# A linear-attention block and a gated MLP on one Trainium2 core: the second half of one weight matrix is loaded on another engine's DMA queue

## The chip, the cores and the metric

The kernel runs on one core of a Trainium2 chip. The metric is the device time of one execution in microseconds (us). Before the change it is 220.55 us, the median of three runs (220.51 to 220.61). A profile of a further execution shows where the time goes.

## What is computed

One layer: a layer norm, then two branches on the same normalised tokens, and a sum with the input. Branch A is linear attention with learned softmax features (32 heads of 16), branch B a gated MLP without an activation function. There are 2048 tokens of width 512, and the MLP is 1792 wide. All tensors are bf16.

```python
x = A_x                                   # [1, 2048, 512]
xn = layernorm(x)                         # mean and variance over the 512
q, k, v = split(xn @ wqkv)                # 32 heads of 16
phi = lambda t: concat(softmax(t @ w_phi), softmax(-(t @ w_phi)))
kv = phi(k).T @ v;  z = phi(k).sum(tokens)
attn = (phi(q) @ kv) / (phi(q) @ z + 1e-6)
mlp = ((xn @ w_gate) * (xn @ w_up)) @ w_down
out = x + attn @ wo + mlp
```

## The kernel before

The tokens are cut into 16 tiles of 128 (`n`), and four tiles make a group (`T`). TensorE (PE) does all projections with 128x512 matmuls; ScalarE (ACT) does the exponentials and many copies out of PSUM; VectorE (DVE) does sums, reciprocals and the products of gate and up; GpSimd (POOL) does the softmax scaling and small scalars; SyncE (SP) only issues DMAs. The order on every engine is written out by hand (`manual_schedule`, L100): each engine executes its instructions in the order of the program text.

All weights are loaded once, at the start, and stay in SBUF. Two engines issue the loads, each on a hardware queue of its own. In the profile q1 is SP's queue and q10 is ACT's.

- On SP (L95 to L97, then L106 to L115): token tile 0 (`dma_x(0, 1)`, "x0" below, 128 KB), token tiles 2 and 3 together (`dma_pair(2)`, "the pair", 256 KB), the second half of the value weights `wv` (contraction chunks 2 and 3, L97, 256 KB), then the first 256 columns of the gate weights `wg` and of the up weights `wu` (256 KB each), `wphi`, the next 384 columns of `wg` and `wu`, a transposing load `wT2` of the key weights (L109), token tiles 4 to 7, the rest of `wg` and `wu`, tiles 8 to 15, `wd` and `wo`.
- On ACT (L103 to L105): after an activation that loads the table, token tile 1 ("x1", 128 KB) and the first half of `wv` (chunks 0 and 1, 256 KB).

The DMAs share eight semaphores in rotation. A DMA whose semaphore is taken by an earlier one waits on the issuing engine until that one has landed. In the program before, `wT2` (L109) waits in this way for the second half of `wv`.

The first four token tiles are treated apart. They are centred by DVE (`sub_sum`), transposed on PE (`lt`), and the value projection of tiles 0, 1 and 2 is cut into two halves (`first_v`, L366 to L369): first the contraction chunks 0 and 1, which need only the first half of `wv`, and later chunks 2 and 3. The text from L399 to L413 sets PE's order: `first_v(0, (0, 1))`, the transposes of tile 2, `first_v(1, (0, 1))`, `first_v(2, (0, 1))`, then `first_v(0, (2, 3))`, which is the first matmul that reads the second half of `wv`, then the transposes of tile 3, the second halves of tiles 1 and 2, and tile 3. The accumulators of tiles 0 and 1 appear as `kv` in the profile (they borrow those two banks), the others as `pv`.

After that PE runs the first MLP units (`ffn`, L278: 4 gate and 4 up matmuls each), the fold of `wphi` into the key weights (`fold`, L230), the key projections, and from tile 4 on the main loop (L447). Tiles 4 to 15 get their normalised transpose `xnT` from ACT and a transposing DMA on SP's queue (`apply` in `ln_block`, L203 to L207), which stands on that queue behind all the weight loads. The first reader of `xnT` for tile 4 is `vproj(4)` (L450).

Of the kernel before, what the change touches and what calls it, by code (L numbers as in the profile page):

```python
# [21 lines left out]
def kernel(  # L22
# [12 lines left out]
    nc = tc.nc  # L35
# [6 lines left out]
    DC = D // P  # L42
# [35 lines left out]
    def dma_x(lo, hi, eng=nc.sync):  # L78
        eng.dma_start(out=xall[:, lo:hi, :], in_=x_view[:, lo:hi, :])  # L79

    def dma_pair(n, eng=nc.sync):
        eng.dma_start(out=xall[:, n:n + 2, :], in_=pair(x_rows, n))  # L82

    def dma_cols(eng, w, src, lo, hi, at=0):
        eng.dma_start(out=w[:, :, lo - at:hi - at], in_=src[:, lo:hi].rearrange("(c p) f -> p c f", p=P))

    def dma_wv(lo, hi, eng):
        eng.dma_start(out=wv[:, lo:hi, :],
                      in_=A_wqkv[lo * P:hi * P, 2 * D:3 * D].rearrange("(c p) f -> p c f", p=P))

    def dma_gu(lo, hi):
        dma_cols(nc.sync, wg, B_w_gate, lo, hi)
        dma_cols(nc.sync, wu, B_w_up, lo, hi)

    dma_x(0, 1)  # L95
    dma_pair(2)
    dma_wv(2, DC, nc.sync)  # L97

    ET = mybir.EngineType
    ctx.enter_context(tc.manual_schedule(engines={ET.PE, ET.DVE, ET.Activation, ET.Pool, ET.SP}))  # L100
# [2 lines left out]
    nc.scalar.activation(out=first[:], in_=ones[:, 0:1], func=AF.Exp, scale=1.0)  # L103
    dma_x(1, 2, nc.scalar)
    dma_wv(0, 2, nc.scalar)  # L105
    dma_gu(0, 2 * P)  # L106
    nc.sync.dma_start(out=wphi[:], in_=A_w_phi.rearrange("(c h) d f -> (h d) c f", c=DC))
    dma_gu(2 * P, 5 * P)
# [429 lines left out]
```

## Time and profile before

| What | Value |
|---|---|
| median of three runs | 220.55 us |
| the profiled execution | 221.2 us |
| its span, from the first to the last instruction | 219.5 us |
| PE busy | 215.7 us, 98% of the span |
| DVE, ACT, POOL busy | 64%, 41%, 34% |
| HBM read / written | 8.67 MB / 2.10 MB |
| packets on SP's queue q1 / ACT's queue q10 | 47952 / 416 |
| granted TensorE clock | 1.0 throughout |

The span is 1.7 us shorter than the time of that execution; the rest lies outside the first and last instruction. PE is busy nearly all the time by this count, but a matmul's recorded end is modelled, so short stalls between matmuls hide in it. They are read from the distance between the starts of matmuls: a 128x512 matmul follows the one before it after 0.216 us when nothing holds it. DMA packets are counted on all 16 DMA engines together; a DMA has landed when each of them has added its one to the DMA's semaphore.

### The profile page before, as it was taken

The numbers are of one execution on the slowest core, as the hardware profiler recorded it, in microseconds if no ns is written. First come the engines' busy times: TensorE is split into PE (matmuls) and PEld (weight loads), VectorE is DVE, ScalarE is ACT, GpSimd is POOL, SyncE is SP. The second block draws the span as 40 slices with busy tenths as digits, with TensorE's granted clock in tenths as the row PEclk, the third lists the DMA queues.
The fourth block names the chain that finished last, engine by engine and source line by source line (L and its number), as shares of the span: only waits on it lengthen the run. The fifth ranks groups of instructions, "written<-read, shape, count | busy, mean of one in ns | idle before, by whom it ended". The sixth has DMA issues, their size and how long they took to land.

```text
span 219.5 us, 3491 instructions
## 1 busy us (share of the span) xinstructions
PE 215.7 (98%) x1291; PEld 103.4 (47%) x1291; DVE 141.1 (64%) x242; ACT 89.2 (41%) x159; POOL 74.1 (34%) x71
## 2 busy tenths in 40 slices
PE   8999999999999999999999999999999999999995
PEld 3444445454444444444554444444444444454443
DVE  4868866786598757667499773197655745454321
ACT  5445586459665875465444222231232322100000
POOL 2450853363348463736135433033023033000000
PEclk9999999999999999999999999999999999999999
DMA  5999997103202231202018445214451431412201
GB/s 189 267 268 365 378 237 147 25 0 51 48 0 49 51 72 23 48 3 48 1 26 97 97 101 115 51 24 96 96 73 26 96 72 28 94 50 72 70 28 48
DMA packets 48385, 19.91 MB, mean 91 GB/s; under 512 B 37488, under 2 KB 48240, under 8 KB 48368
## 3 DMA queue, kind: packets, MB, share of 16 engines
q1 hardware_dynamic: 47952, 19.29, 38.8%
q10 hardware_dynamic: 416, 0.39, 0.5%
q8 instruction: 10, 0.16, 0.3%
q14 instruction: 7, 0.06, 0.1%
HBM read 8.67 MB, written 2.10 MB: 49 GB/s over the span
## 4 chain that ended last, share of the span: by engine, by line
PE 95%; DMA 3%; SPq 0%; DVE 0%; issue 0%
PE g L287 22%; PE fin L303 22%; PE u L291 22%; PE fin L306 6%; PE k L249 6%; PE q L249 6%; PE pv L249 5%; DMA wv<-in_A_wqkv_dram 3%; PE kv L343 2%; PE ab L477 2%; PE pq L238 1%; PE kv L249 0%; SPq L82 0%; SPq L79 0%; DVE o_sb L313 0%
## 5 line engine op out<-in xcount | busy, mean ns | idle before, releaser
L291 PE MATMUL u<-xnT,wu 128*128 128x512 bf16 x224 | 57.5, 379 | 0.0
L287 PE MATMUL g<-xnT,wg 128*128 128x512 bf16 x224 | 57.5, 379 | 0.0
L295 DVE TENSOR_TENSOR hT<-u,g_sb 128x512 bf16<-128x512 f32 x56 | 37.0, 666 | 24.2 <-PE u L291 16.0
L266 POOL TENSOR_TENSOR phiq<-e,rsum 128x1024 bf16<-128x1024 f32 x16 | 30.9, 1933 | 63.5 <-DVE rsum L264 56.0
L262 DVE TENSOR_REDUCE sums<-e 128x64 f32<-128x1024 f32 x32 | 38.9, 1216 | 20.3 <-ACT e L259 20.3
L294 ACT CAST g_sb<-g 128x512 bf16<-128x512 f32 x56 | 32.9, 587 | 46.8 <-PE g L287 46.6
L303 PE MATMUL fin<-wd,hT 128*128 128x512 bf16 (+2 forms) x238 | 51.1, 366 | 0.0
L266 POOL TENSOR_TENSOR phik<-e,rsum 128x1024 bf16<-128x1024 f32 x16 | 30.9, 1932 | 40.0 <-DVE rsum L264 34.0
L291 PEld LDWEIGHTS <-wu 128*128 128x128 bf16 x224 | 21.9, 98 | 26.4
L303 PEld LDWEIGHTS <-hT 128*128 128x128 bf16 x238 | 22.4, 98 | 24.7
L287 PEld LDWEIGHTS <-wg 128*128 128x128 bf16 x224 | 21.1, 98 | 23.9
L249 PEld LDWEIGHTS <-xnT 128*128 128x128 bf16 x192 | 17.4, 98 | 18.5 <-ACT xnT L219 0.7
L313 DVE TENSOR_TENSOR o_sb<-fin,xall 128x512 bf16<-128x512 f32 (+2 forms) x13 | 8.5, 651 | 20.5 <-PE fin L306 20.5
L264 DVE RECIPROCAL rsum<-sums 128x64 f32<-128x64 f32 x32 | 17.7, 553 | 3.1
L306 PE MATMUL fin<-wo,oT 128*128 128x512 bf16 (+2 forms) x68 | 16.6, 366 | 0.0
L249 PE MATMUL k<-W1k,xnT 128*128 128x512 bf16 x64 | 16.4, 379 | 0.0
L249 PE MATMUL q<-W1q,xnT 128*128 128x512 bf16 x64 | 16.4, 378 | 0.0
L258 ACT ACTIVATE e<-q 128x512 f32<-128x512 f32 x12 | 7.2, 597 | 22.2 <-PE q L249 22.2
L249 PE MATMUL pv<-wv,xnT 128*128 128x512 bf16 x56 | 14.4, 379 | 0.0
L490 DVE TENSOR_TENSOR otok<-ab,rden 128x512 bf16<-128x512 f32 x16 | 11.1, 692 | 0.6
L335 ACT CAST vt<-pv 128x512 bf16<-128x512 f32 x12 | 7.0, 587 | 10.2 <-PE pv L249 10.2
L166 DVE BATCH_NORM_STATS2 stats<-xall 128x6 f32<-128x512 bf16 x16 | 10.6, 664 | 0.0
(62 smaller groups left out, 131.8 us busy)
## 6 DMA issues: line engine op xcount, KB each, us to landing
out_dram<-o_sb SPq DMA_DIRECT2D x15, 128.0 KB, 2.0
wd<-in_B_w_down_dram SPq DMA_DIRECT2D x1, 1792.0 KB, 15.7
xall<-in_A_x_dram SPq DMA_DIRECT2D x1, 1024.0 KB, 11.8
wg<-in_B_w_gate_dram SPq DMA_DIRECT2D x1, 640.0 KB, 9.1
wu<-in_B_w_up_dram SPq DMA_DIRECT2D x1, 640.0 KB, 10.2
xall<-in_A_x_dram SPq DMA_DIRECT2D x1, 512.0 KB, 4.4
wg<-in_B_w_gate_dram SPq DMA_DIRECT2D x1, 512.0 KB, 5.2
wu<-in_B_w_up_dram SPq DMA_DIRECT2D x1, 512.0 KB, 6.2
```

The source lines that it names most:

```text
L166: nc.vector.bn_stats(out=stats[:], in_=xall[:, n, :])
L249: nc.tensor.matmul(ps, lhsT=xnT[:, j, n * P:(n + 1) * P], rhs=w[:, j, :], start=(j == 0), stop=(j == DC - 1))
L262: nc.vector.tensor_reduce(out=sums[:], in_=ev, axis=AX.X, op=ALU.add)
L264: nc.vector.reciprocal(out=rsum[:].rearrange("p a b -> p (a b)"), in_=sums[:])
L266: nc.gpsimd.tensor_tensor(out=phi[:].rearrange("p g (x f) -> p (g x) f", f=DH), in0=ev, in1=rsum[:].to_broadcast((P, 2 * H, DH)), op=ALU.mult)
L287: nc.tensor.matmul(gps, lhsT=wg[:, c, f * P:(f + 1) * P], rhs=xnT[:, c, T * TT:(T + 1) * TT], start=(c == 0), stop=(c == DC - 1))
L291: nc.tensor.matmul(ups, lhsT=wu[:, c, f * P:(f + 1) * P], rhs=xnT[:, c, T * TT:(T + 1) * TT], start=(c == 0), stop=(c == DC - 1))
L294: nc.scalar.copy(out=g_sb[:], in_=gps)
L295: nc.vector.tensor_tensor(out=hTs[T][:, f, :], in0=ups, in1=g_sb[:], op=ALU.mult)
L303: nc.tensor.matmul(ps, lhsT=hTs[T][:, f, t4 * P:(t4 + 1) * P], rhs=wd[:, f, lo:lo + w], start=(f == 0), stop=False)
L306: nc.tensor.matmul(ps, lhsT=oTs[n][:, c, :], rhs=wo[:, c, lo:lo + w], start=False, stop=(c == DC - 1))
L490: nc.vector.tensor_tensor(out=o_tok[:].rearrange("p (b h d) -> p b h d", b=2, d=DH), in0=abv[:, :, :, 0:DH], in1=rden[:].to_broadcast((P, ...
```

## The change

The load of the second half of `wv` is taken from SP's queue, where it stood third, and put on ACT's queue, behind the first half. Nothing else in the text changes. PE, DVE and POOL have the same instructions in the same order. ACT has one DMA more, SP one less. Because the eight semaphores are handed out in order, some of them change hands: `wT2` (L109 before) now waits for the first part of `wg` to land instead of the second half of `wv`.

```diff
     dma_x(0, 1)
     dma_pair(2)
-    dma_wv(2, DC, nc.sync)
...
     dma_x(1, 2, nc.scalar)
     dma_wv(0, 2, nc.scalar)
+    dma_wv(2, DC, nc.scalar)
     dma_gu(0, 2 * P)
```

## Prediction

> **What bounds the kernel now.** I read the chain of waits first, since PE's 98% hides short stalls.
>
> ```profile
> 7.58 0.04 issue
> 7.62 0.59 PE kv L249 x2
> ...
> 28.97 0.25 PE kv L343 x8
> ...
> 33.54 0.26 PE kv L343 x8
> 33.80 1.03 PE pv L249 x4
> 34.83 0.86 PE k L249 x4
> ```
>
> Columns: start, length, what. From 7.62 us to the end the chain is PE alone, and before that it is the landing of `wv`. Two places are not at full pace. At 7.62 PE starts `first_v(0, (2, 3))`, 0.04 us after the second half of `wv` has landed (7.58). The matmul before it started at 7.18, so without a wait the next would have started at 7.18 + 0.22 = 7.40: PE loses 0.22 us. At 33.80 four matmuls of `vproj(4)` take 1.03 us where four others take 0.86: 0.17 us lost. That matmul reads `xnT` of tile 4, whose transposing DMA was issued at 26.93 and landed 6.8 us later, at 33.73. Everywhere else in the chain the pieces have their nominal length, so the time after 33.8 us is fixed work. Hence the end is set by the later of two things: PE's own arrival at `vproj(4)` (33.63 now) and the landing of `xnT` 4 (PE goes on at 33.80).
>
> The second thing to read is the start of the two queues.
>
> ```profile
> 0.79 0.39 SPq L79 DMA_DIRECT2D xall<-in_A_x_dram  x1
> 0.84 0.39 ACTq L79 DMA_DIRECT2D xall<-in_A_x_dram  x1
> 1.24 0.41 SPq L82 DMA_DIRECT2D xall<-in_A_x_dram  x1
> 1.27 0.46 ACTq L88 DMA_DIRECT2D wv<-in_A_wqkv_dram  x1
> 1.70 0.43 SPq L88 DMA_DIRECT2D wv<-in_A_wqkv_dram  x1
> 2.18 0.47 SPq L85 DMA_DIRECT2D wg<-in_B_w_gate_dram  x1
> ```
>
> So the order of issue is x0, x1, the pair, `wv` first half, `wv` second half, `wg`. Now the packets per queue, in the stretches 3.25 to 3.5, 4.0 to 4.25 and 4.75 to 5.0 us (packets, MB, their time as a share of 16 engines), and all packets from 5.5 to 6.5 us:
>
> ```profile
> q1 hardware_dynamic: 48, 0.10, 100.8%
> q10 hardware_dynamic: 1, 0.00, 0.2%
> ```
> ```profile
> q10 hardware_dynamic: 95, 0.10, 108.3%
> ```
> ```profile
> q1 hardware_dynamic: 70, 0.07, 79.7%
> ```
> ```profile
> DMA packets 558, 0.29 MB, mean 292 GB/s; under 512 B 16, under 2 KB 558, under 8 KB 558
> ```
>
> At 3.25 SP's queue moves the pair and ACT's queue stands still, although the first half of `wv` had been issued by 1.73. At 4.0 only ACT's queue moves, although SP's third load had been issued by 2.13. From 4.75 only SP's moves. The two queues are not served side by side here: the DMAs are served one after another in the order in which they were issued, whichever queue they are on, even where the issues are 0.03 us apart (1.24 and 1.27).
>
> ```profile
> wv<-in_A_wqkv_dram SPq DMA_DIRECT2D x1, 256.0 KB, 5.9
> wg<-in_B_w_gate_dram SPq DMA_DIRECT2D x1, 256.0 KB, 6.3
> ```
>
> The last column is us from issue to landing: `wv` second half 1.70 + 5.9 = 7.6, `wg` first part 2.18 + 6.3 = 8.48.
>
> **The change, part by part.** *SP's third issue goes.* It took 0.43 us and a gap of 0.05, so every later issue on SP that is not held by a wait comes 0.48 us earlier: `wg` at 1.70 instead of 2.18, `wu` at 2.21, `wphi` at 2.76, and so on. No engine waits for these issues themselves.
>
> *ACT gets a third issue* at 1.27 + 0.46 + 0.04 = 1.77, for about 0.46 us (the row of the first half, same shape). The next thing in ACT's order is the first `junk` sum, which starts at 3.58 when x1 has landed. The issue ends at 2.23, so 1.35 us of waiting covers it; the one activation before it runs at 2.08 behind the table load. Cost nothing; without that cover it would be 0.46 us on the sum of tile 1.
>
> *The order of service changes.* This is the term that decides. `wg` is now issued at 1.70 and the second half of `wv` at 1.77. By the order seen above `wg` is served first and `wv` second. Both are 256 KB, so they swap places: `wv` lands where `wg` landed, at 8.48, and PE resumes 0.04 us later, at 8.52 instead of 7.62, **+0.90 us**. A second way gives the same: 256 KB (0.262 MB) of `wg` at the 292 GB/s of the stretch 5.5 to 6.5 take 0.90 us, and that is what is put ahead of `wv`. Queued behind the waiting matmul on PE are the transposes of tile 3, the rest of the value projections and all MLP units; ACT, DVE and POOL follow PE there (the copy of tile 3's transpose at 8.47, the value copies from 9.39), so the whole front moves by 0.90. `wg`, needed by PE at 9.78 (then 10.68), lands about 7.6. No loss there.
>
> *What takes some of it back.* At 33.63 + 0.90 = 34.53 PE comes to `vproj(4)`, whose `xnT` landed at 33.73. The 0.17 us that PE now waits there vanish. So the end moves by 0.90 - 0.17 = **+0.73 us**, if the landing of `xnT` 4 stays. It stands behind the same weight bytes on SP's queue. `wT2` waits for whichever of the two loads is served first: `wv` before (landed 7.58, `wT2` issued at 7.59), `wg` after (again about 7.6), so the rest of the stream starts as before. And it may come 0.8 us later without being felt.
>
> *Bounds.* The landing is the uncertain number, since it goes by the slowest of 16 DMA engines. The trace records each increment of a DMA's semaphore: for the second half of `wv` 15 of the 16 had come by 6.45 and the last at 7.58; for `wg` 7.64 and 8.48. If that one late engine were not late, `wv` in second place would land at 7.64, PE would resume at 7.68, and PE's 0.06 us would vanish in the wait at 33.6: no change. If it lost another 0.4 us (a single 1 KB packet of it took 0.50 us), `wv` would land at 8.88 and PE resume at 8.92: 1.30 later, less the 0.17, +1.13. On the side of a gain: PE cannot resume before 7.40 nor save more than the 0.17 at 33.8, together 0.39 us. I take 8.48, the nearest row: same bytes, same place in the order, same engines.
>
> **Against a rule of the Trainium skill.** In "DMA: Bandwidth & Descriptors", section "Queues, rings and completion order", each DMA engine takes turns between the queues that have work, a packet from one, then a packet from the other. The rows above (48 packets against 1, then 95 against none) disagree with it in these first microseconds. By that rule the second half of `wv` would follow the first half at once and share the engines with `wg`, and the time would be that of the second rival.
>
> **The sum.** Against the profiled execution: 221.2 + 0.73 = 221.93, with a span of 220.2. The runs' median lies 0.65 below that execution, so the forecast is 220.55 + 0.73 = **221.28 us**, +0.33%. I count 0.2% (0.44 us) as what a measurement of this kernel can tell from no change.
>
> **The rivals.** *The late engine, or a tie of issues, hides it.* If the late engine of the profile is not late in other runs, or if ACT's issue slips ahead of SP's (0.07 us apart) so that `wv` keeps its place and the change does nothing, `wv` lands between 6.5 and 8.0, PE resumes by 8.04 at the latest, and the time is 220.55 to 220.8. For it: only one engine of 16 was late. Against: SP led ACT in both earlier pairs of issues (0.05 and 0.03 us), and ACT's issue of 256 rows takes longer than SP's of 128.
>
> *Both queues work side by side (not slower).* If `wv` on ACT's queue is not held by `wg`, it starts when the first half ends (4.5), and its 16 packets per engine of 46 ns alternate with 28 ns packets of `wg`: 16 x 0.074 = 1.2 us, done at 5.7, so that PE resumes at 7.40 to 7.62. That alone gains nothing, since PE then waits longer for `xnT` 4. But between 4.5 and 5.5 the engines were busy for only 0.75 of the time at 237 GB/s; two queues would fill that, the stream of loads would end about 0.3 us earlier, and the end with it: 220.2 to 220.55. It decides once the queues are served together; against it stand the rows above, for it that the engines did have gaps while one queue had them alone.
>
> *More is lost.* The late engine gets later because `wg`'s 32 packets on each engine pass before `wv`'s 16, and `wv` lands at 9 or after: PE resumes at 9.05, +1.43 - 0.17 = +1.26, 221.8. For it: one packet of that engine took 0.50 us. Against: the same bytes were carried by 8.48.
>
> **How the numbers follow.** The forecast gets 0.55, the hidden case 0.15, the side-by-side case 0.20, the greater loss 0.10. Of the forecast's share 0.05 may end below the bound of 0.2% (`wv` landing before 8.2). So slower is 0.50 + 0.10 = 0.60; same is 0.05 + 0.15 + most of the side-by-side case (0.15) = 0.35; faster by over 0.2% is 0.05, since the waits named allow 0.39 us. The range must reach into the side-by-side case and take in the upper bound of the landing: 220.55 + 1.13 = 221.68. I take 220.25 to 221.7; the forecast's own is 220.9 to 221.7.
>
> **What would show it.** In the profile after: `wv`'s ACT issue at about 1.77 and a landing 6.7 us later; q1 alone moving 512-byte packets of `wg` from 4.4 us and q10 again from about 5.4; `first_v(0, (2, 3))` at 8.5; `vproj(4)` at nominal length (0.86) about 34.5; a span near 220.2. Wrong if q10 goes on without a break after 4.5 us, if PE resumes before 7.8, or if a wait at `vproj(4)` remains.

## The result, and the profile after

The changed kernel takes 221.37 us (median of six runs, 220.88 to 221.85) against 220.56 us for the kernel before beside it (six runs, 220.27 to 220.75). The ratio is 1.0034 with a 95% interval of 1.0021 to 1.0048: 0.34% slower, where 221.28 us had been forecast.

The profiled execution of it, however, was its fastest: 220.88 us, with a span of 219.2 us, 0.3 us shorter than that of the profile before. So the first reading of this profile has to be that it does not show the loss. Its chain of waits (start, length, what):

```profile
1.27 4.04 DMA wv<-in_A_wqkv_dram
5.31 0.04 issue
5.35 1.01 PE kv L249 x2
6.36 0.33 PE tp L218 x4
6.69 0.43 PE kv L249 x2
7.12 0.53 PE pv L249 x2
7.64 0.43 PE kv L249 x2
...
33.41 0.26 PE kv L343 x8
33.66 0.86 PE pv L249 x4
```

The chain begins with the first half of `wv` (issued at 1.27), not the second. `first_v(0, (2, 3))`, the piece at 7.64, follows the matmuls before it without a gap, and `vproj(4)` at 33.66 has its nominal 0.86 us: the wait of 0.17 us is gone. The issues:

```profile
1.25 0.41 SPq L82 DMA_DIRECT2D xall<-in_A_x_dram  x1
1.71 0.43 SPq L85 DMA_DIRECT2D wg<-in_B_w_gate_dram  x1
2.18 0.51 SPq L85 DMA_DIRECT2D wu<-in_B_w_up_dram  x1
...
1.27 0.98 ACTq L88 DMA_DIRECT2D wv<-in_A_wqkv_dram  x2
```

SP issues `wg` at 1.71. ACT's two loads of `wv` are merged into one row, 0.98 us from 1.27 on; the second is issued at 1.76, behind `wg`. The DMA rows of the page (last column: median us from issue to landing):

```profile
wv<-in_A_wqkv_dram ACTq DMA_DIRECT2D x2, 256.0 KB, 4.6
...
wg<-in_B_w_gate_dram SPq DMA_DIRECT2D x1, 256.0 KB, 5.4
```

The two halves took 4.0 and 5.2 us, so the second landed at 6.92 us and `wg` at 7.14. PE wanted the second half at 7.48. Whether this kernel loses time is decided within about a microsecond that differs from one execution to the next, and one profile is not enough to see it.

### The profile page after: what moved, and what is told of

The parts are those of the page before. It is cut to its first block, busy times and chain, and to the rows that moved or that the text cites. A ratio compares the mean times of both kernels' runs of the same rounds, so it can differ in the third digit from the quotient of the medians.

```text
span 219.2 us, 3467 instructions
## 1 busy us (share of the span) xinstructions
PE 214.2 (98%) x1267; PEld 103.3 (47%) x1291; DVE 141.2 (64%) x242; ACT 89.0 (41%) x159; POOL 74.1 (34%) x71
## 4 chain that ended last, share of the span: by engine, by line
PE 96%; DMA 2%; issue 1%; ACT 0%; DVE 0%
PE u L291 22%; PE fin L303 22%; PE g L287 22%; PE fin L306 6%; PE q L249 6%; PE k L249 6%; PE pv L249 6%; PE ab L477 2%; PE kv L343 2%; DMA wv<-in_A_wqkv_dram 2%; PE kv L249 1%; PE pq L238 1%; PE tp L218 0%; ACT L102 0%; DVE o_sb L313 0%
## 5 line engine op out<-in xcount | busy, mean ns | idle before, releaser
L291 PE MATMUL u<-xnT,wu 128*128 128x512 bf16 x221 | 56.8, 379 | 0.2
L287 PE MATMUL g<-xnT,wg 128*128 128x512 bf16 x213 | 56.3, 379 | 0.6
L249 PE MATMUL k<-W1k,xnT 128*128 128x512 bf16 x61 | 15.8, 379 | 0.0
```

What stands on the lines that cost most here:

```text
L249: nc.tensor.matmul(ps, lhsT=xnT[:, j, n * P:(n + 1) * P], rhs=w[:, j, :], start=(j == 0), stop=(j == DC - 1))
L287: nc.tensor.matmul(gps, lhsT=wg[:, c, f * P:(f + 1) * P], rhs=xnT[:, c, T * TT:(T + 1) * TT], start=(c == 0), stop=(c == DC - 1))
L291: nc.tensor.matmul(ups, lhsT=wu[:, c, f * P:(f + 1) * P], rhs=xnT[:, c, T * TT:(T + 1) * TT], start=(c == 0), stop=(c == DC - 1))
```

## The experiments

"The half" below is the second half of `wv`. All times are medians; "beside it" is the kernel before on the same chip. The column "PE starts" is the start of the first matmul that reads the half.

| Kernel | us (runs) | beside it | ratio, 95% interval | profiled execution: us, the half lands, PE starts |
|---|---|---|---|---|
| before, first profile | 220.55 (3) | | | 221.2, 7.58, 7.62 |
| before, second | 220.66 (12) | 220.72 | 1.0007 (0.997 to 1.0043) | 220.33, 6.45, 6.95 |
| before, third | 220.77 (12) | 220.67 | 1.0006 (0.9973 to 1.0038) | 220.43, 5.81, 7.02 |
| changed, first | 221.37 (6) | 220.56 | 1.0034 (1.0021 to 1.0048) | 220.88, 6.92, 7.48 |
| changed, second | 221.51 (12) | 220.72 | 1.002 (0.9987 to 1.0053) | 221.67, 8.23, 8.28 |
| changed, third | 221.26 (12) | 220.67 | 1.0027 (1.0011 to 1.0042) | 221.23, 7.76, 7.80 |
| `wg` first, both on SP | 220.75 (12) | 220.72 | 0.999 (0.9957 to 1.0023) | 220.74, 7.27, 7.32 |
| changed, `wphi` ahead of `wg` | 220.92 (12) | 220.72 | 1.0007 (0.9977 to 1.0038) | 221.63, 8.20, 8.24 |
| the mirror: `wg` on ACT | 220.98 (12) | 220.74 | 1.0008 (0.9981 to 1.0036) | 220.22, 6.28, 6.82 |
| changed, SP held | 224.25 (5) | 220.74 | 1.0161 (1.0123 to 1.02) | 225.2, 6.09, 7.12 |
| changed, tile 3 first | 221.19 (12) | 220.74 | 1.0028 (1.0001 to 1.0054) | 220.63, 7.41, 7.46 |
| before, tile 3 first | 220.61 (12) | 220.74 | 0.9991 (0.9971 to 1.0012) | 220.44, 6.64, 7.20 |
| changed, PE filled | 221.86 (8) | 220.67 | 1.0055 (1.0036 to 1.0073) | 221.32, 7.70, 7.93 |
| before, PE filled | 221.80 (10) | 220.67 | 1.0045 (1.0017 to 1.0073) | 222.45, 6.74, 9.04 |

A few executions stray far: five of the 24 in the second and third rows took 222.5 to 223.6 us, while none of the 30 of the changed kernel took more than 222.27. With tile 3 first it is the other way round (two of twelve of the changed kernel at 222.62 and 223.06, none of the other), so nothing says that the change has a part in it. No profile caught one; what is late in them stays open.

### More profiles of both kernels

No edit: the changed kernel and the kernel before were run again, twice each.

> The changed kernel once more, for a second profile and more times, since the profiled execution of it (220.88) was the fastest of its six. Theory A (wg's first part, issued 0.06 us ahead, is served ahead of wv's second half, so the half lands later, and how much later PE feels depends on how late the slowest of 16 DMA engines is in that execution): median 221.1 to 221.7, and a profile of an execution near 221.4 shows wv's second half landing at 7.9 to 8.5 and a gap before first_v(0, (2, 3)). Rival B (the first half of wv, which shares the engines with wg's first packets, lands late and PE starts its first projection late): the gap is before first_v(0, (0, 1)), 0.5 us or more. Rival C (not the loads at all, but PE's clock or a later place): neither gap, and the difference appears after 10 us.

> The kernel before once more, same place. All theories: ratio 1.000, median about 220.5; it shows how far one profile of the same program differs from the next. Theory A expects wv's second half to land between 6.4 and 7.6 here, earlier than in the changed kernel run beside it.

> The changed kernel a third time, beside the two with the extra matmuls and on the same chip: 221.2 to 221.6. Theory A': wv's second half lands at 6.9 to 8.3, and the gap before first_v(0, (2, 3)) is that landing less PE's arrival (6.9 to 7.5, by when the clock rises).

> The kernel before a third time: 220.5 to 220.8, with wv's second half landing at 6.3 to 7.6 and a gap of at most 0.3 us.

The chain of the changed kernel's second profile, an execution of 221.67 us:

```profile
1.27 0.46 ACTq L88
1.73 0.03 issue
1.76 6.48 DMA wv<-in_A_wqkv_dram
8.23 0.04 issue
8.28 0.59 PE kv L249 x2
...
217.25 0.29 DVE o_sb L313
```

And of the kernel before, second profile, an execution of 220.33 us:

```profile
6.58 0.53 PE pv L249 x2
7.11 0.43 PE kv L249 x2
7.54 0.22 PE tp L218 x4
...
215.93 0.29 DVE o_sb L313
```

In the first the half, issued at 1.76, lands 6.48 us later, and the matmul behind it starts at 8.28. The one before it had started at 7.25 and would have been followed at 7.47: PE waits 0.81 us. In the second there is no wait. (The chain gives 7.11 for that matmul because it counts a pipelined matmul by its end; its start is 6.95.) The last rows are the first part of the last output, and they close the account: from the start of that matmul to this row it is 217.25 - 8.28 = 208.97 us in the one and 215.93 - 6.95 = 208.98 in the other. The third profiles give 216.78 - 7.80 and 215.99 - 7.02, again 208.98 and 208.97, and the changed kernel's first 216.46 - 7.48 = 208.98. Only the first profile of the kernel before has 216.76 - 7.62 = 209.14, which is its wait of 0.17 us at `vproj(4)`. So, apart from that wait, nothing after 8.3 us differs in these six profiles. The difference is the start of one matmul: 7.48, 8.28 and 7.80 (mean 7.85) after the change, 7.62, 6.95 and 7.02 (mean 7.20) before. The 0.65 us between the means fit the +0.5 to +0.8 us of the medians. The time of the execution follows that start too. Time less start is 213.38 to 213.43 us in five of these profiles, and also in those with PE filled, with `wg` first, with `wg` on ACT and with `wphi` ahead of `wg` (see the table); it is 213.58 in the first of the kernel before.

Two things add up in a start: when PE has done the matmuls before it, and how long it then waits. PE could have started at 7.40, 6.95 and 7.02 before and at 7.48, 7.47 and 7.08 after, on average 0.22 us later. The waits are 0.22, 0 and 0 before and 0, 0.81 and 0.72 after, on average 0.44 us longer. The later arrival goes with the first half of `wv`, which landed at 5.31, 5.06 and 5.42 after the change and at 4.99, 4.90 and 5.36 before, and with the pace of PE (see the end). With three profiles each it can't be told from scatter. Of the four forecasts one was missed: in the third profile of the kernel before the half landed at 5.81, ahead of the 6.3 to 7.6 that were expected.

### Filling PE's wait

```diff
+        warm_up(5)
         first_v(0, (2, 3))
```

> The changed kernel with five matmuls that nobody reads (5 x 0.216 = 1.08 us on PE) put ahead of first_v(0, (2, 3)), that is, into the place where PE waits for wv's second half. Theory A' (PE's wait there is the whole loss): PE reaches that matmul 1.08 us later, when the half has landed in nearly every execution, so only the part of the 1.08 that is not waiting is added: 221.5 to 221.9, the same as the kernel before with the same five matmuls (difference below 0.3). Rival (the loss is elsewhere: PE's clock, the first half, or the stream of loads after 8 us): the 0.8 us between the two kernels stays, 222.2 to 222.6.

> The kernel before with the same five matmuls in the same place. Both theories: 220.65 + 0.8 to 1.08 = 221.4 to 221.7, since PE hardly waits there before. It is the yardstick of the run beside it.

The five matmuls feed nothing. They lift the kernel before from 220.77 to 221.80 us, by 1.03 us, nearly their full 1.08. They lift the changed kernel from 221.26 to 221.86, by only 0.60. With them the two kernels differ by 0.06 us, without them by 0.49 on the same chip. The chain of the changed kernel, filled:

```profile
7.00 1.09 PE warm L321 x5
8.09 0.43 PE kv L249 x2
...
216.91 0.29 DVE o_sb L313
```

The half landed at 7.70 here, while PE was still on the extra matmuls, and PE went on at 7.93 without a gap. (The chain gives the end-based 8.09 for that start.) This is the firmest of the experiments, as it rests on eighteen runs of two programs that differ in the change alone: the loss goes when PE's wait for the half is filled, and no other effect of the change is left over that the runs can tell. They can't tell a few tenths of a microsecond, as the intervals of the two filled kernels (1.0036 to 1.0073 and 1.0017 to 1.0073) show. The filled kernel before, at 221.80, is 0.1 us above its forecast.

### The order of service alone

```diff
+    dma_cols(nc.sync, wg, B_w_gate, 0, 2 * P)
     dma_wv(2, DC, nc.sync)
...
-    dma_gu(0, 2 * P)
+    dma_cols(nc.sync, wu, B_w_up, 0, 2 * P)
```

> The kernel before, both halves of wv on their old queues, but wg's first part issued ahead of wv's second half on SP. Theory A (order of service, not the queue): as slow as the changed kernel or slower, since wg now stands wholly ahead of wv: +0.6 to +1.1 us, 221.1 to 221.6, wv's second half landing at about 8. Rival B (the first half of wv suffers from wg beside it): also slow, but with the gap before first_v(0, (0, 1)). A third, that the cost is in ACT's queue itself: no change, 220.5.

The half stays on SP's queue but stands behind `wg`. It landed at 7.27 and PE waited 0.57 us in that profile, yet the median is that of the kernel before (three of the twelve runs took 221.7 to 221.9). The wait cost little because PE was early, at 6.75: it started on the half at 7.32, only 0.12 us behind the mean start of the kernel before. The theory as first put, that being served behind `wg` is by itself worth +0.6 us or more, falls; the interval, up to 1.0023, leaves room for less.

### The half issued ahead of `wg`, and the mirror of the change

```diff
+    nc.sync.dma_start(out=wphi[:], in_=A_w_phi.rearrange("(c h) d f -> (h d) c f", c=DC))
     dma_gu(0, 2 * P)
-    nc.sync.dma_start(out=wphi[:], in_=A_w_phi.rearrange("(c h) d f -> (h d) c f", c=DC))
```

> The changed kernel with SP's issue of wphi (0.5 to 1.1 us) put ahead of wg's, so that ACT issues wv's second half at 1.76 before SP issues wg at about 2.3. Theory A: the order of service is that of before again, wv's second half lands at 5.7 to 7.5 and the loss is gone: 220.3 to 220.6. Rival B: wv's first half lands no later than before (5.0), loss gone too. Third (the cost is in ACT's queue): still about 221.3.

ACT issued the half at 1.77 and SP `wg` at 2.18. Still the half landed at 8.20 in the profile, and PE waited 1.2 us. The runs split: six of twelve at 220.59 to 220.79, five at 221.63 to 222.01. So the half can be late even when it is issued ahead of `wg`, and the forecast (220.3 to 220.6, a landing by 7.5) was missed. The edit doesn't put the half first, though: `wphi` was issued at 1.70, ahead of it, as 512 packets of 32 bytes, and itself landed only at 7.96.

```diff
     dma_wv(0, 2, nc.scalar)
-    dma_gu(0, 2 * P)
+    dma_cols(nc.scalar, wg, B_w_gate, 0, 2 * P)
+    dma_cols(nc.sync, wu, B_w_up, 0, 2 * P)
```

> The mirror of the change: wv's second half stays on SP's queue and wg's first part goes on ACT's queue behind the first half of wv, so the same two loads run on two queues, with wv issued first (1.70 against 1.76). If sharing the engines with the other queue is what makes wv late (theory A'): the second half lands at 7.0 to 8.2, and the time is 220.9 to 221.5. If the order of issue decides (theory A as first put): wv is served first as before and lands at 5.7 to 7.5: 220.4 to 220.7. If ACT's queue itself is slow: wg is late instead, but PE wants it only at about 9.5, so 220.4 to 220.7 as well with wg landing at 8.5 or later.

The half on SP, first in order, with `wg` beside it on ACT: it landed at 6.28, no gap, and the median is 0.24 us above the one beside it, within the interval of no change. The profile speaks for the order of issue, but it is of one of the two fastest executions (220.22). The median, 220.98, lies just within the forecast for sharing (220.9 to 221.5). The run doesn't decide between the two.

### The half alone on ACT's queue

```diff
+    held = consts.tile([P, 1, 16], BF16)
+    nc.sync.dma_start(out=held[:], in_=wv[:, 2:3, 0:16])
     dma_gu(0, 2 * P)
```

> The changed kernel with a small transfer on SP, ahead of wg, that reads wv's second half and so holds SP's queue until that half has landed: the second half has the DMA engines for itself on ACT's queue. Theory A' (sharing): it lands by 5.5 to 6.2 and PE has no gap before first_v(0, (2, 3)), but wg, issued some 4 us late, lands after 9 and PE waits there, and the loads after it are late too: 221.5 to 224. If ACT's queue itself is slow or the stalls come without any sharing: wv's second half still lands after 6.8.

Packets of both queues in the stretch 5.0 to 5.5 us (packets, MB, their time as a share of the 16 engines), first in the changed kernel's second profile:

```profile
q10 hardware_dynamic: 73, 0.07, 52.0%
q1 hardware_dynamic: 114, 0.06, 39.0%
```

then with SP held, where the half is almost through and SP's queue is empty:

```profile
q10 hardware_dynamic: 32, 0.03, 15.2%
```

Alone, the half landed at 6.09, as forecast, and 15 of its 16 engines were done by 5.68. In the changed kernel's second profile the median engine was done at 6.57 and the last two at 8.22 and 8.23. ACT's queue is therefore not slow in itself; SP's loads ahead of it and beside it make the half late. The price of holding SP, 3.5 us, is the late `wg` and all that comes after it: the issue of `wg` moved to 6.70, and PE waited several times between 9 and 24 us; that is a little more than the 224 us that were expected at most.

### Other work ahead of the wait

```diff
-        first_v(0, (2, 3))
         lt(3)
+        first_v(0, (2, 3))
         first_v(1, (2, 3))
```

> The changed kernel with the transposes of tile 3 moved ahead of first_v(0, (2, 3)) on PE (4 transposes of 0.055 us), so that PE's wait for wv's second half has other work in front and ACT's copy of tile 3's transpose (0.59 us) runs in the shadow of the wait. Theory A' (the loss is PE's wait for wv's second half, which on ACT's queue shares the engines with SP's loads and is late on the slowest of them): 0.2 to 0.8 us of the loss come back, 220.7 to 221.3. Rival B (first half late) or a place after 10 us: nothing comes back, 221.4 to 221.6.

> The kernel before with the same move on PE. Theory A': before, the second half lands close to when PE wants it (6.45 and 7.58 us in two profiles, wanted at 6.95 and 7.40), so little is to be had: 220.4 to 220.7, ratio 0.998 to 1.000. Rival B: same as before.

The changed kernel came to +0.45 us against the one beside it, where it had +0.79 and +0.59 without the move; the ratios (1.0028 against 1.002 and 1.0027) don't tell them apart. Inconclusive. On the kernel before the move gives -0.13 us, within the interval of no change; nothing that was run beats the kernel before by more than the runs can tell.

## Why the prediction was right, and where its steps were not

**What bounds the kernel: right, with one term that belonged to one execution.** The time is set by when PE starts on the half, and the 208.98 us after that are fixed. The wait at `vproj(4)`, and so the credit of 0.17 us, was there in the first profile of the kernel before only: in its second and third `xnT` of tile 4 landed at 32.64 and 32.24, ahead of PE. In those two executions there was nothing to give back. (The chain has another piece over its nominal length, the gate matmuls at 15.91 with 0.97 us for 0.86; the fixed 208.98 us show that it costs the same in every profile.)

**The issues: right.** SP's issues moved up (`wg` 1.71, `wu` 2.18, `wphi` 2.73) and ACT's third, at 1.76, took 0.49 us and held nobody.

**The order of service: right in sign, wrong as a rule.** The prediction had the half wait until all of `wg` was served and land at 8.48 instead of 7.58, with `wg` in the old place at about 7.6. Measured were 6.92, 8.23 and 7.76 after the change (mean 7.64) against 7.58, 6.45 and 5.81 before (mean 6.61): 1.03 us later, where 0.90 was forecast, with both ends nearly a microsecond lower. The first profile of the kernel before had been an execution at the slow end of its runs (221.2 us where most are 220.2 to 221.0). And the two loads did not swap places: `wg` landed at 7.14, 7.76 and 7.55, within 0.5 us of the half, and in the first profile after it. In the changed kernel's second profile the queues moved in the stretch 4.5 to 5.0

```profile
q1 hardware_dynamic: 197, 0.10, 69.6%
q10 hardware_dynamic: 24, 0.02, 12.8%
```

where ACT's queue with SP held, and so alone, moved

```profile
q10 hardware_dynamic: 175, 0.17, 96.0%
```

so `wg` does go first for a while. But from 5.0 on both move, 114 packets against 73. By then some 246 of the 512 packets of `wg` had gone (49 from 4.0 to 4.5, then 197), so what the half shares the engines with is first the rest of `wg` itself, and then what SP has issued behind it. This sharing is what the rule of the Trainium skill says that the prediction set aside ("DMA: Bandwidth & Descriptors", section "Queues, rings and completion order": an engine takes turns between its queues). From 5.0 us on the trace agrees with it; before, with 24 packets against 197, it does not.

How much each part adds is seen best on the eighth of the 16 engines to finish the half, which scatters less than the last. It was done at 5.65, 5.48 and 5.70 before and at 6.48, 6.57 and 6.78 after, 1.00 us later on average. Behind `wg` on one queue it was done at 6.36, ahead of `wg` on another queue at 5.98, and with no other load at 5.43. These are single profiles, but by them both the order and the sharing make the half late. In the times neither part alone shows clearly (220.75 and 220.98 us, both together 221.26 to 221.51); PE doesn't want the half before 6.75 to 7.5, so a small delay is not felt, and the intervals of the two, up to 1.0023 and 1.0036, leave room for part of the loss, the second for all of it. Why some engines are over a microsecond behind the rest in one execution and not in the next stays open; no run could set a single engine's pace.

**PE's delay: right within the spread, and in part by luck.** Forecast +0.90 less 0.17. Measured 0.65 us between the mean starts; the medians moved by +0.49 to +0.81. The landing moved by more than forecast (1.03), and the credit of 0.17 was not there, but 0.38 us of the shift went into slack, which the prediction had at nothing: before, the half lands on average 0.59 us ahead of the matmul that reads it (6.61 against 7.20), and after the change 0.21 us. The one profile that the prediction was made from had a wait there instead. That the errors cancel to within 0.1 us is luck. By the prediction's own signs the first profile after the change counts against it (PE resumed at 7.48, before 7.8), the second and third do not (8.28 and 7.80); the start at 8.5 and the span of 220.2 us were nearly reached in the second alone (8.28 and 220.0).

**`wT2` and the stream of loads: right.** `wT2` was issued at 7.16, 7.78 and 7.57, when `wg` had landed, and no wait at `vproj(4)` appeared, as PE came to it at 33.5 to 34.3 and `xnT` had landed at 32.1 to 33.2.

**The rivals.** The late engines are real: in the second profile the last two were 0.75 us behind the rest (8.22 and 8.23 after 7.47), in the first none was (6.92 after 6.89), and the executions took 221.67 and 220.88 us. The case of queues side by side happened in part, and did not bring the gain worked out for it: the half landed over a microsecond after the 5.7 that it gave. The greater loss, a landing at 9 us or later, was in no profile.

## What to carry to other kernels

In this kernel the load that PE wants within microseconds of its issue was done earliest where the loads that are needed later stood behind it on its own queue or were held until it was through (5.43 to 5.70 us on the median engine). On the second queue it started after what the other engine had issued 0.05 us earlier, and then shared the DMA engines with the rest of that (6.48 to 6.78). For another kernel this is a thing to test and not a rule. Where a kernel hangs on the landing of one early load, take several profiles before believing a wait that one of them shows, and test it by filling the wait with work that does nothing: what the fill doesn't cost is the wait. Read the landing on the median engine as well as on the last, since it shows a shift through the scatter.

## What was not expected of the hardware

The same program runs PE at two paces, and goes from the one to the other at a point that differs between executions. In the first profile of the kernel before the first two matmuls of `first_v` start 0.43 us apart and take 1.06 us together, in the second they start 0.22 apart and take 0.59:

```profile
5.21 1.06 PE L249 MATMUL kv<-wv,xnT 128*128 128x512 bf16 x2
```
```profile
4.98 0.59 PE L249 MATMUL kv<-wv,xnT 128*128 128x512 bf16 x2
```

In four of the fourteen profiles PE was still at the slow pace at that point (twice the changed kernel, once the kernel before, once the one with `wphi` first); in the others it had doubled by then. The views print a granted clock of 1.00 for these microseconds too, but the clock record in the trace only begins later: at 6.41 us after the first instruction in the first profile of the kernel before and at 4.16 in the second, and at about these points the starts of the matmuls draw together. In the twelve profiles that have such a record it begins at 3.60 to 6.54 us. PE came to the half at 7.05 to 7.48 in the four slow ones and at 6.75 to 7.12 in six fast ones with the same work ahead, so the pace accounts for part of a spread that is as large as the cost of the change; the landing of the first half of `wv` moves it as well. The Trainium skill ("TensorE: Matmul & The Clock Gate", section "Part 1: The HAM clock gate") says that the clock is raised by a free-running window and so at a point that shifts from run to run; the two rows agree with that. It puts the shift at ±0.5 us; here the records begin up to 2.9 us apart.

The landing of one 256 KB load scatters by 1.3 to 1.8 us between executions of one program (5.81 to 7.58 before, 6.92 to 8.23 after), set by the slowest few of the 16 DMA engines: the eighth scatters by 0.2 to 0.3 us. In one profile it hit the first half of `wv` instead: with the fill on the kernel before, that half landed at 6.30 instead of about 5.0, and the execution took 222.45 us against a median of 221.80.
